# Another written order of the steps, and the second PSUM bank of two inverse quarters taken from the three-bank ring

## The chip, the core and the metric

The kernel runs on one core of a Trainium2 chip. The metric is the time on the device of one execution, in microseconds, as the median of several runs. Five engines run side by side, each through its own list of instructions in a fixed order: TensorE (PE; its weight loads are shown as PEld), VectorE (DVE), ScalarE (ACT), GpSimd (POOL) and SyncE (SP, which here only issues DMAs). An instruction starts when the one before it on its engine lets it and the semaphores that it waits for are there.

## The reference

The input is layer-normed to `xn` (2048 rows of 448), and two branches are added to it. Branch A is a state space layer, done as a long convolution; branch B sends each row to the best of 64 x 64 experts in each of 16 heads.

```
xn  = layernorm(x)
# A: D=448 channels, N=256 states
P   = exp(dt*A[:, :, None] * l)                    # l = 0..2047
K   = einsum("dn,dnl,dn->dl", C, P, dt*B).real
y   = irfft(rfft(pad(xn)) * rfft(pad(K)))[:2048] + xn * Dskip
# B: 16 heads, 64x64 experts, the best one of each head
q   = einsum("nd,dhc->nhc", xn, w_q)
s1, s2 = q[..., :256] @ k1.T, q[..., 256:] @ k2.T
e   = argmax(s1) * 64 + argmax(s2)
act = gelu(einsum("nd,nhd->nh", xn, u[e]))         # the softmax over one candidate is 1
out = x + y + einsum("nh,nhd->nd", act, v[e])
```

## The kernel before

**Scores.** `combine` folds each head's `w_q` with the keys (L916, transposes at L931) into a score matrix `W`. For each of 16 tiles of 128 rows, `score` transposes the normed tile (L1000, evicted at L1003), multiplies it with `W` in four quarters (`sc_p`: L1019, L1030) and finds the best key of each head on DVE: the maximum of a row at L1045, a mask at L1052, a tree of minima at L1062 to L1068. A pair of tiles shares the last small steps, and the indices go through DRAM (L1114, L1121).

**Tables.** `batch` makes the powers of the state space layer for 8 channels: exponentials from PE and ACT (L617, L628), phases on DVE (L653), sines on ACT (L668 to L674), and four products on DVE (L699 to L705, the steps `s4_v`). `products` then takes the sum over the states (`k1`, L721, step `s4_k1`), evicts it (L729; the skip term is added at L732), and transforms it (`k3`, L742, step `s4_k3`) into `VK`, evicted at L746. There are 56 batches.

**Convolution.** `conv` handles the channels in chunks of 128, 128, 128 and 64, each in four quarters of frequencies. In the last chunk a quarter is a product with `g` (`cv1`, L824), a multiplication on DVE (`cv3`, L832, two instructions), the inverse (`cv5`, L876) into two PSUM banks, their eviction (`cv6`, L889, one for each bank) and two stores to DRAM (`cv7`, L895). `final` loads the result back across quarters (L1221), does the last product (`f_p`, L1234), evicts it (L1240) and adds it to the output with a DMA that accumulates (L1245).

**Experts.** For each tile, `experts` gathers 16 pieces of expert rows with an indirect DMA (L1148, POOL's queue), multiplies each with the matching rows of `xn` and sums on DVE (the dots, L1156; the rows come from the DMA at L1138 into four buffers called `xr`), puts the results through a gelu (L1163 to L1172, ACT and DVE in turn), spreads them into a matrix `A` (L1179) and sums the weighted expert rows on PE (L1191, step `e_p`), which also frees the gathered buffers. The sum is evicted (L1198) and added to the output (L1201).

**Order.** Nothing is scheduled at run time. All steps are put into streams (one for each kind of work) and the string `ORDER` names, one character a step, which stream gives the next step. Each engine's list is that order cut to the engine. Buffers are rings: a step takes a slot of a ring (`take`) and a later step gives it back (`give`), first freed, first taken. PSUM has eight banks: the ring `kv` with three (tables, `combine`, `f_p`), the ring `s2` with three (scores, `cv1`, one half of an inverse), and one each for `tp` (transposes, the other half of an inverse) and `po` (experts). 25 buffers of 128 x 1024 named `q` are shared by nearly everything that is loaded or gathered.

Of the kernel before, what the change touches and what calls it, by code (L numbers as in the profile page):

```python
# [89 lines left out]
def ac(n):  # L90
    return 55 + 0.833 * n
# [24 lines left out]
class Plan:  # L116
# [65 lines left out]
    "4414Z44HHH04H114116444242462II2IIII2II2I2I2I222I222222JLJ72HMKHH4H234LML477788ML443K44878M44Z44NI4ICCOPC5N4441DDHE7E77CD"  # L182
    "CHI7I9IIIIIIIIEJ9L7H7DM9FFCEL446CD744EF8JDMK4H79749C7EIC7LF8DE8CF7IDMFDF777897R4N445EII9IEDCFF8I7IR76E4CIFD7444ED4SI7RCF"
    "ESD44FAC499AAIEL848MFDZCCZASHESDHEDFFIEF9HRR9ROHAAaQxZPRISISRRISTURUIIIUIIUJUcIIdSSRRJHGIQxegZbHISGHOShBfHPKISSSTUUUUUUU"
    "UUVWWRRRRXSSRROSSfYYyyQyyPyRySIISfhLySTxfRgQNMRxLJhhRgfIhMUUSSUzUzSUzz!RhROyyyIS#!Izh#hSP$z$%yyyyzz!h#SSg!R#I$$%yyTLRRJh"
    "izUczKUSUzUIUzIhMR!#z#h!$SLU$fz%NRUhMRIzOfUSUIfhzVI!hQSS#SgWIW#SyP!hGTRhcyiiyy$$%Jgxf&RxUxixzzaUiSRNhyzXGhRyzKfy!#Kj#h!S"
    "$z$iUSzRSS%RdOPUyzSzL!SMRyz#U!(hLy#yyTzi$$%hyyykMhiYyieRQUUzizzLy!Rj#zMh#dLiz!$hZHex$%khUSzH!iMZRLblfHM#iLM!HUiUlSgRxhjR"
    "#fiNSihgKf$S$OhfcS%IUIIyyyySIxJhSPUTQUzzIxgLyfNyzUhQRzUhIURIUMhk!U#m#IzLmI!&N$nj$h%zIyyyyyhMRSIhzzynh!liKkYz##!hi$S$SUzz"
    "R%VzgZSINZih!#zh!lyHyHyhHJR1ROSP#m$$%SHfizxJSTgIhhyILIfRzIzgIfWQ!MyLRfhUIW#njIi!zfUhhxmy#US$xcxkUyzU$(zdRizyy%nMiRyyeiSy"
    "h!#li#IL&h!hhIhM$zSj$ySURziISzhRX%zIigIiabiOhkhPgK!R#SShzQhYJlgR#LUf!J$$%UyzyizfZHizUyyTM!SfhNZmR#fYzRS!fSzRmhyVyhWjh#Wz"  # L190
    "$SzRinHH$%hSHk!ny#OKUyIS#SKUjylihIUP!yL$iUMTIhckUNxRL$%IUlUzMLIhg&MRhaILxURmxxKyQzfhISfhUIzzzUSfIgyzyyizfhMRzIiISKh!X#gR"
    "RUy#fh!$S$hdOUIyi%%jzSSSinUhhiPhhmknRibUiyRTJRRiUilyyhehhjgSiSzzUUzzRhhyyfzzUgSUiSySROzQVyShhfPQSk!##gh(hfi!$fJRLj$yyTU%"
    "lfUWkMlcxiUhaRx%yymRLyyySimh&hMLjiUyhhnhniSUiRRgRSUzUxNhzSUWNzMOkhUxzzzzzfh!SyYgfyyPYQ#iSiyS!h#zfL$hz$Rig%%RfRfizzyyzljM"
# [1117 lines left out]
```

## Time and profile before

| what | us |
|---|---|
| median of 3 runs | 757.4 |
| lowest and highest | 754.84 and 757.84 |
| the profiled execution's own time | 760.1 |
| its span, first to last instruction | 758.3 |
| busy in it: PE, DVE, ACT, POOL | 646.2, 659.6, 548.3, 359.9 |

A busy share is an average over stages. The prediction below cuts the span into stretches, looks for the engine that is full in each, and asks which engine waited for which. In a line of a group, the numbers behind the bar are its busy time, the mean length of one in ns, and the idle time of the engine just ahead of it, with what ended most of that. In a timeline the first two numbers are the start and the length, and what stands in brackets is the idle time before and what ended it. "x2" counts instructions.

### The profile page before, as it was taken

Reading aid. Unit: us, or ns where it says so; the run is one execution under the profiler, and the core shown is the slowest. Engines: PE = TensorE matmul, PEld = TensorE weight load, DVE = VectorE, ACT = ScalarE, POOL = GpSimd, SP = SyncE. Lnnn points to the kernel's source line nnn. Section 1 sums busy time; section 2 is a strip of 40 time slices with the busy share of each in tenths; the row PEclk is TensorE's granted clock in tenths of the full one; section 3 lists DMA queues with packets and bytes.
Section 4 is the critical chain, followed back from the end, with each engine's and each line's share of the span. In section 5 each row is a group of like instructions: output and inputs, shape, how many; then the busy total and the mean of one; then the engine's idle time right before and its main releaser. Section 6 shows DMA issues by size and latency. Waiting matters only on the chain.

```text
span 758.3 us, 19601 instructions
## 1 busy us (share of the span) xinstructions
PE 646.2 (85%) x7628; PEld 357.3 (47%) x7628; DVE 659.6 (87%) x1595; ACT 548.3 (72%) x1089; POOL 359.9 (47%) x307
## 2 busy tenths in 40 slices
PE   1999999999998999999899776559997577999892
PEld 0334333344443444443466653336764344676761
DVE  5695557999998999999899999999999989999740
ACT  4686425638896676846668897988889898999630
POOL 2100015653464345554624676786646387616323
PEclk9999999999999999999999997687996776899995
DMA  8999619898988858878997999999989999969889
GB/s 271 331 372 339 233 43 344 268 368 275 330 293 272 244 200 246 247 244 250 306 321 234 319 333 300 323 343 335 301 267 355 276 300 322 258 218 273 298 170 123
DMA packets 118085, 211.29 MB, mean 279 GB/s; under 512 B 38824, under 2 KB 93096, under 8 KB 117928
## 3 DMA queue, kind: packets, MB, share of 16 engines
q0 software_dynamic: 31232, 124.80, 52.2%
q1 hardware_dynamic: 86760, 85.24, 35.4%
q8 instruction: 60, 0.98, 0.5%
q14 instruction: 33, 0.27, 0.1%
HBM read 180.38 MB, written 33.29 MB: 282 GB/s over the span
## 4 chain that ended last, share of the span: by engine, by line
DVE 38%; PE 29%; ACT 15%; DMA 9%; issue 7%; POOL 1%; SPq 1%; POOLq 0%; DVEq 0%; ACTq 0%
PE s L1019 9%; DVE q L1156 9%; DVE mg L705 4%; DVE ph L653 4%; DVE zi L701 4%; PE kv L721 3%; PE kv L916 3%; DMA xr<-xn_d 2%; DVE q L858 2%; ACT CS L668 2%; ACT CS L671 2%; DVE mx L1045 2%; DVE zi L699 2%; ACT CS L674 2%; PE s L1030 2%
## 5 line engine op out<-in xcount | busy, mean ns | idle before, releaser
L1148 POOL DMA_INDIRECT q<-in_uv_dram,ig x256 | 311.9, 1218 | 308.6 <-PE po L1191 93.8
L1019 PE MATMUL s<-q,xt 128*128 128x512 f32 x384 | 178.9, 605 | 3.4 <-ACT xt L1003 2.8
L1156 DVE SCALAR_TENSOR_TENSOR q<-q,xr 128x448 f32<-128x448 f32 x256 | 152.9, 619 | 6.7 <-DMA q<-in_uv_dram,ig 3.7
L1019 PEld LDWEIGHTS s<-q,xt 128*128 128x128 f32 x384 | 69.0, 190 | 92.2 <-issue 85.5
L721 PE MATMUL kv<-mg 128*32 128x64 f32 x1792 | 65.8, 243 | 12.5 <-DVE mg L705 6.9
L1191 PE MATMUL po<-q,A 128*32 128x448 f32 x512 | 67.0, 618 | 10.7 <-DVE A L1179 5.0
L628 ACT ACTIVATE mg<-kv 128x512 f32<-128x512 f32 x112 | 63.5, 604 | 16.4 <-PE kv L617 15.8
L701 DVE TENSOR_TENSOR zi<-mg,CS 128x1024 f32<-128x1024 f32 x56 | 68.4, 1221 | 0.0
L705 DVE TENSOR_TENSOR mg<-mg,CS 128x1024 f32<-128x1024 f32 x56 | 68.2, 1219 | 0.0
L721 PE MATMUL kv<-zi 128*32 128x64 f32 x1792 | 65.7, 240 | 0.2
L668 ACT ACTIVATE CS<-ph 128x1024 f32<-128x1024 int32 x56 | 62.7, 1120 | 3.8 <-DVE ph L653 3.8
L653 DVE CUSTOM_DVE_ANT_0 ph<-st,ph 128x512 uint16<-128x512 uint16 (+2 forms) x84 | 65.1, 775 | 0.2
L674 ACT ACTIVATE CS<-CS,halfpi 128x1024 f32<-128x1024 f32 x56 | 64.5, 1152 | 0.9
L721 PEld LDWEIGHTS kv<-mg 128*32 128x32 f32 x1792 | 47.3, 123 | 33.4 <-issue 14.0
L671 ACT ACTIVATE CS<-ph 128x1024 f32<-128x1024 int32 x56 | 62.7, 1120 | 0.0
L617 PE MATMUL kv<-lc,rt 32*128 32x512 f32 x112 | 39.9, 542 | 26.5 <-ACT mg L628 17.0
L1045 DVE TENSOR_REDUCE mx<-s 128x8 f32<-128x512 f32 x64 | 43.8, 685 | 18.2 <-PE s L1030 13.8
L765 PE MATMUL tp<-q,f 128*128 128x448 f32 x64 | 34.6, 625 | 20.0 <-DMA f<-in_f_dram 14.0
L721 PEld LDWEIGHTS kv<-zi 128*32 128x32 f32 x1792 | 50.2, 125 | 0.8 <-issue 0.7
L881 PE MATMUL s<-q,e 64*128 64x256 f32 x192 | 46.7, 394 | 0.4 <-DVE q L858 0.3
L881 PE MATMUL tp<-q,e 64*128 64x256 f32 x192 | 46.6, 394 | 0.5 <-ACT q L889 0.5
L742 PE MATMUL kv<-f,kt 128*64 128x128 f32 x448 | 38.8, 309 | 9.4 <-ACT mg L628 8.6
(208 smaller groups left out, 1282.4 us busy)
## 6 DMA issues: line engine op xcount, KB each, us to landing
q<-in_wq_dram SPq DMA_DIRECT2D x32, 448.0 KB
xr<-xn_d SPq DMA_DIRECT2D x64, 224.0 KB
vu_d<-q SPq DMA_DIRECT2D x64, 112.0 KB
q<-vu_d SPq DMA_DIRECT2D x12, 512.0 KB
t_d<-q SPq DMA_DIRECT2D x24, 256.0 KB
q<-t_d SPq DMA_DIRECT2D x12, 512.0 KB
q<-in_uv_dram,ig POOLq DMA_INDIRECT x256, 7.1
q<-in_x_dram SPq DMA_DIRECT2D x16, 224.0 KB
```

Source lines behind the costliest of these rows:

```text
L653: s.nc.vector.tensor_tensor(out=rw(n, 2 * n), in0=rw(0, n), in1=o["st"][:, k, b0:b0 + 2].rearrange("p b h m x -> p (b h m x)")[:, None].to ...
L668: s.nc.scalar.activation(CS[:, 1].rearrange("p (m r x) -> p m r x", r=16, x=2), four(s.ph), AF.Sin, scale=SC)
L671: s.nc.scalar.activation(B["CS"][:, 0].rearrange("p (m r x) -> p m r x", r=16, x=2), four(s.ph), AF.Abs)
L674: s.nc.scalar.activation(B["CS"][:, 0], B["CS"][:, 0], AF.Sin, scale=-SC, bias=s.halfpi)
L701: V.tensor_tensor(out=zi[:, 512:], in0=mg[:, 512:], in1=CS[:, 1], op=ALU.mult)
L705: V.tensor_tensor(out=mg[:, 512:], in0=mg[:, 512:], in1=CS[:, 0], op=ALU.mult)
L721: s.nc.tensor.matmul(kp[32 * c:32 * c + 32, 64 * gi:64 * gi + 64], T[ri][:, 1024 + m:1056 + m], view(T[ri], m, [[512, 2], [1, 32]]), start ...
L881: s.nc.tensor.matmul(Q["ip", h][:, 2 * w * x:2 * w * x + 2 * w], s.e[r, k], Q["c", x][r, :, ab, ri], start=(i == 0), stop=(i == 3))
L1019: s.nc.tensor.matmul(B["sc", q].rearrange("p a b -> p (a b)"), B["xt"][:, i], w, start=(q % 2 == 0 and i == 0), stop=(q % 2 == 1 and i == 2))
L1148: s.nc.gpsimd.indirect_dma_start(out=ue, out_offset=None, in_=s.io["uv"], in_offset=bass.IndirectOffsetOnAxis(ap=s.IDX[t][:, c, g:g + 1].b ...
L1156: s.nc.vector.scalar_tensor_tensor(Q["ue", g, c][:, :D], Q["ue", g, c][:, :D], 1.0, B["xr", c], op0=ALU.mult, op1=ALU.mult, accum_out=Q["d ...
L1191: s.nc.tensor.matmul(B["po"][32 * c:32 * c + 32, :D], Q["A"][:, g - g0, c], Q["ue", g, c][:, D:], start=(g == 0), stop=(g == 3))
```

## The change

In the last chunk (`last`), the quarters 1 and 3 take the second bank of their inverse from the ring `kv` instead of `tp`; quarters 0 and 2, and all quarters of the other chunks, are as before. The number of instructions stays as it is, and so does the arithmetic. The string `ORDER` is replaced by another permutation of the same steps; line numbers from there on are two higher (L1191 is now L1193).

```diff
 ORDER = (
-    "4414Z44HHH04H114116444242462II2IIII2II2I2I2I222I222222JLJ72HMKHH4H234LML477788ML443K44878M44Z44NI4ICCOPC5N4441DDHE7E77CD"
+    "041HH4HH222I2II2II22I44I1I4ZI1I41I1IJJ4446H724K22K22222222LMLMHHH4L772M4L678848I5I74834M444CC14ODPDI34444CIEEIDNIIII4Z7C"
...
-            def c5(Q=Q):
+            sec = "kv" if last and q % 2 else "tp"
+
+            def c5(Q=Q, sec=sec):
                 for h in range(2):
-                    Q["ip", h] = s.pst([128, 4 * w], ("s2", "tp")[h], "ip")
+                    Q["ip", h] = s.pst([128, 4 * w], ("s2", sec)[h], "ip")
...
-            m = p.add("cv5", "PE", 36.0 * w, c5, deps=[v, s.C["e"]], take=("i1", "tp", "tq"), give=("cA",) if last else ("cA", "cB"))
+            m = p.add("cv5", "PE", 36.0 * w, c5, deps=[v, s.C["e"]], take=("i1", sec, "tq"), give=("cA",) if last else ("cA", "cB"))
...
-                a = p.add("cv6", "ACT", ac(4 * w), c6, deps=[m], give=(("i1", "tp")[h],))
+                a = p.add("cv6", "ACT", ac(4 * w), c6, deps=[m], give=(("i1", sec)[h],))
```

What this does to the lists is shown at three places.

**PE, the end of the last chunk's inverses.** `L876` (now `L878`) is the inverse of a quarter, `s_` and `tp_` or `kv_` its two banks, `L1191` (now `L1193`) the sum over the last tile's experts, `L1234` (now `L1236`) the last product of the chunk before. Before:

```order
L876 MATMUL tp_110<-q_79,e 128x256
L1191 MATMUL po<-q_96,A 32x448 [waits DMASW1_49]
L1191 MATMUL po<-q_91,A 32x448 [waits DMASW3_49]
L1191 MATMUL po<-q_87,A 32x448 [waits DMASW4_49]
L1191 MATMUL po<-q_98,A 32x448 [waits DMASW5_49]
L1191 MATMUL po<-q_93,A 32x448 [waits DMASW6_49,DVE_49]
L1191 MATMUL po<-q_84,A 32x448 [waits DMASW7_49]
L1191 MATMUL po<-q_103,A 32x448 [waits DMASW0_49]
L1191 MATMUL po<-q_92,A 32x448 [waits DMASW1_49]
L876 MATMUL s_108<-q_101,e 128x256
L876 MATMUL tp_110<-q_101,e 128x256 [waits Activation_49]
```

And now:

```order
L878 MATMUL s_107<-q_92,e 128x256
L878 MATMUL tp_110<-q_92,e 128x256
L1236 MATMUL kv_106<-q_98,q_95 32x128 [waits DMAHW1_49]
L1236 MATMUL kv_106<-q_98,q_95 32x128 x15
L878 MATMUL s_109<-q_99,e 128x256 [waits DVE_49,Activation_49]
L878 MATMUL kv_105<-q_99,e 128x256 [waits Activation_49]
```

Between the third and the fourth inverse there stood eight expert sums; now one last product of the chunk before stands there, and those sums come behind the fourth inverse, which writes a bank of `kv`.

**DVE, the last dots of tile 6.** `L1156` (now `L1158`) is a dot, `L1052`, `L1062` and `L1065` (now two higher) work on scores, `L699` to `L705` are products of the tables. Before, from the 109th to the 112th of the kernel's dots:

```order
L1156 SCALAR_TENSOR_TENSOR q_80,dot<-q_80,xr 128x448 [waits DMASW1_49]
L1156 SCALAR_TENSOR_TENSOR q_87,dot<-q_87,xr 128x448 [waits DMASW2_49]
L1156 SCALAR_TENSOR_TENSOR q_81,dot<-q_81,xr 128x448 [waits DMAHW6_49,DMAHW5_49,DMAHW7_49,DMAHW4_49,DMASW3_49]
L1052 TENSOR_TENSOR q_90<-s_108,mx 128x512 [waits DVE_49,PE_49]
L649 TENSOR_SCALAR ph<-tpl 128x2x2x16 [waits Activation_49]
L649 TENSOR_SCALAR ph<-tpl 128x2x2x16
L732 TENSOR_TENSOR kt<-kv_104,dsk 128x2 [waits Activation_49]
L699 SCALAR_TENSOR_TENSOR zi<-mg,CS 128x512
L1156 SCALAR_TENSOR_TENSOR q_102,dot<-q_102,xr 128x448 [waits DMASW4_49]
```

And now, the same four:

```order
L1158 SCALAR_TENSOR_TENSOR q_99,dot<-q_99,xr 128x448 [waits DMASW7_49]
L1067 TENSOR_TENSOR q_79<-q_79 128x32x32 [waits DVE_49]
L1158 SCALAR_TENSOR_TENSOR q_95,dot<-q_95,xr 128x448 [waits DMAHW2_49,DMAHW1_49,DMAHW7_49,DMAHW0_49,DMASW0_49]
L1158 SCALAR_TENSOR_TENSOR q_80,dot<-q_80,xr 128x448 [waits DMASW1_49]
L1067 TENSOR_TENSOR q_79<-q_79 128x32x16 [waits DVE_49]
L703 TENSOR_TENSOR mg<-mg,CS 128x512
L1158 SCALAR_TENSOR_TENSOR q_88,dot<-q_88,xr 128x448 [waits DMASW2_49]
```

The fourth dot, on `q_88`, now has its gather in a buffer that the first expert sums of the same tile free; before, its buffer came from an older score step.

**DVE, the step from tile 9 to tile 10.** Here the first `xr` buffer is used again: its load for tile 10 can be issued once tile 9's 13th dot is through. `L653` are phases, `L1108`, `L1111`, `L1166` to `L1179` small steps of scores and gelu. Before, the last rows ahead of tile 10's first dot (26 rows stand between the two dots):

```order
L653 ISA ph<-st,ph 128x512 [waits DVE_49]
L1175 TENSOR_TENSOR dw<-dot,ig 128x8
L701 TENSOR_TENSOR zi<-mg,CS 128x1024
L653 ISA ph<-st,ph 128x1024 [waits DVE_49]
L1172 SCALAR_TENSOR_TENSOR th<-th,dw 128x8 [waits DVE_49,Activation_49]
L1179 TENSOR_TENSOR A<-mask,th 128x256 [waits DVE_49]
L703 TENSOR_TENSOR mg<-mg,CS 128x512
L653 ISA ph<-st,ph 128x2048
L705 TENSOR_TENSOR mg<-mg,CS 128x1024
L1156 SCALAR_TENSOR_TENSOR q_103,dot<-q_103,xr 128x448 [waits DMAHW2_49,DMASW1_49]
```

And now, with 20 rows between the two:

```order
L701 TENSOR_TENSOR zi<-mg,CS 128x1024
L1110 RECIPROCAL rcg<-top 128x32
L1168 SCALAR_TENSOR_TENSOR x_4610<-x_4610,dot 128x8 [waits Activation_49]
L653 ISA ph<-ph,st 128x256 [waits DVE_49]
L703 TENSOR_TENSOR mg<-mg,CS 128x512
L653 ISA ph<-st,ph 128x512 [waits DVE_49]
L1177 TENSOR_TENSOR dw<-dot,ig 128x8
L653 ISA ph<-st,ph 128x1024 [waits DVE_49]
L705 TENSOR_TENSOR mg<-mg,CS 128x1024
L1174 SCALAR_TENSOR_TENSOR th<-th,dw 128x8 [waits DVE_49,Activation_49]
L1181 TENSOR_TENSOR A<-mask,th 128x256 [waits DVE_49]
L1158 SCALAR_TENSOR_TENSOR q_84,dot<-q_84,xr 128x448 [waits DMAHW2_49,DMASW0_49]
```

A phase step (`L653` 128x2048) and a set of table products went from ahead of the dot to behind it.

More of the change, by code (lines that the diff above doesn't have):

```diff
@@ new lines @@
+    "IIH74C974FFHIEJLDJCEM5HD97HE6D748LM9F7C8FD74F4E7CN44F4ED4ECIF9787LC8NF4R4C48DMR4ZI4I444EDDC9FECZK4FECZRDFE9I9H7A4HK4H79D"
+    "DILSxI988CHFEMDSIEFF4CEDFEF7RRROIIIQP7Q9IS7SxRNIJxGJ76A7779A7AAABcIaSISSGTUIURRRSUUUSRROSPSSSSTUUUUUUUUIUdeRZRSgIRHHVWWR"
+    "XYyyyyIhIISRROHhSSHIISIyxyIIIYISQPgRIySLbffTRhhgRMILyIRIfMIhfJIUIUISSUUzzzz!#U!hRKROI#ShzSz$fPz$z!hSh#SQ!STy%#hyJhi$$Ryg"
+    "yyy%hyyhRLRMzUUSRSUUfJLUzGUfzRzSRzhUzS!#z#N!$zcQx!SMJhiSO#g!$yS#U$%U$cPVTfiR%RWhyhxgyzyzyyxyxyaUzWNUfUSzR&!SU#f!U#SRhz$h"
@@ L212 @@
+    "phhqiftzi!qgrp#hhpqrxoygfo#ftq!vrp$hfh$k%ixywjhflrsqiixhhhiirklpiij%ghhqhkithhfrliuvpgtqphxmfihqfgrifr&njfzushhhhizhhomo"
+    "hvnthkjmvhiiyztiiilkiu-ljm(iuiynzmynknymyjwwnlzklyywmmyyzyynnzpzzzyyp!pyr#!#$$%rszztrtz)zzrz!##!$$rr)pstt*stut*+(,+))urr"
+    "stt*%%*,%+&,(uu+,)*+,)))*+,*+,*+,")
 class Kernel:
```

47 lines of the change are left out of this document (20 added, 27 removed).

## The prediction

> **What bounds the kernel now.** I read the page first, then the stretches of the span, then DVE's waits. The page's first lines:
>
> ```profile
> span 758.3 us, 19601 instructions
> PE 646.2 (85%) x7628; PEld 357.3 (47%) x7628; DVE 659.6 (87%) x1595; ACT 548.3 (72%) x1089; POOL 359.9 (47%) x307
> ```
>
> PE and DVE are nearly alike over the span, so I cut it where the scores end. The last score matrix product starts at 383 us; in the view by stretches the columns are busy time and count for PE, PEld, DVE, ACT, POOL, then granted clock, DMA share and GB/s:
>
> ```profile
> 383.43 2.84 PE L1019 MATMUL s<-q,xt 128*128 128x512 f32 x6
> ...
> 0.00:20.00 20.00, 3.69 (x4) 1.00 (x4) 10.03 (x35) 8.74 (x21) 5.69 (x17) 1.00 0.86 263
> 20.00:40.00 20.00, 19.01 (x65) 8.15 (x65) 15.11 (x22) 12.13 (x23) 2.08 (x1) 1.00 0.95 336
> 40.00:60.00 20.00, 19.00 (x83) 7.68 (x84) 19.79 (x26) 17.27 (x46) 2.08 (x1) 1.00 1.02 389
> 100.00:140.00 40.00, 38.72 (x119) 15.45 (x120) 29.96 (x78) 18.16 (x48) 18.08 (x16) 1.00 0.70 230
> 140.00:300.00 160.00, 154.45 (x1191) 66.86 (x1190) 154.30 (x432) 115.54 (x254) 78.07 (x70) 1.00 0.85 280
> 300.00:386.00 86.00, 80.89 (x687) 35.87 (x685) 81.88 (x201) 53.06 (x111) 42.72 (x35) 1.00 0.84 268
> 386.00:500.00 114.00, 87.86 (x1545) 60.06 (x1548) 111.83 (x265) 98.08 (x175) 73.47 (x57) 0.88 0.94 305
> 500.00:600.00 100.00, 80.16 (x1412) 56.09 (x1400) 96.69 (x227) 88.39 (x148) 62.28 (x50) 0.84 0.99 315
> 600.00:720.00 120.00, 101.58 (x1934) 73.27 (x1936) 111.30 (x246) 108.69 (x187) 64.14 (x52) 0.85 0.90 276
> 720.00:730.00 10.00, 10.00 (x224) 8.21 (x224) 8.36 (x26) 2.12 (x8) 0.00 (x0) 1.00 0.51 130
> ```
>
> To 140 us PE is full (38.72 of the last 40) and DVE is not (29.96). From 140 to 386 both are: DVE lacks 5.7 and 4.1 us, PE 5.6 and 5.1. From 386 to 720 DVE alone is full: it lacks 2.2, 3.3 and 8.7 us, PE far more. So from 140 us on the span is DVE's work plus DVE's waits, some 24 us of them (5.7 + 4.1 + 2.2 + 3.3 + 8.7), and the new order holds the same work. What it can win or lose is in those 24 us, in the start, and in the tail behind DVE's last work. DVE's waits, in total, times, longest:
>
> ```profile
> DVE kt L732 <- ACT kt L729: 7.1, 7, 3.2
> DVE q L1156 <- DMA q<-in_uv_dram,ig: 3.7, 3, 2.2
> DVE q L1156 <- DMA xr<-xn_d: 2.9, 1, 2.9
> DVE zi L699 <- ACT CS L668: 1.9, 2, 1.3
> ```
>
> **The bank alone: 0.** The group of the fourth bank's products in the last chunk has no idle time ahead of it:
>
> ```profile
> L876 PE MATMUL tp<-q,e 64*128 64x256 f32 x32 | 8.0, 389 | 0.0
> L889 ACT ACTIVATE q<-s 128x256 f32<-128x256 f32 x4 | 1.5, 384 | 11.9 <-PE tp L876 11.9
> ```
>
> PE is busy throughout 720 to 730 with other steps between two inverses, which hide the eviction of `tp`. If that cover went, a quarter would wait for two evictions of 0.38 us; the new list puts quarters 1 and 3 on `kv`, so it cannot go there. Taking a `kv` bank could hold up a last product of the chunk before, which comes behind and has time until the final loads. Both ends near nothing; I take 0. What is left is the order.
>
> **The start: -0.5 (between -1.7 and 0).** PE starts when the matrix `f` is there:
>
> ```profile
> 6.86 0.47 SPq L454 DMA_DIRECT2D pv<-in_A_im_dram  x1
> 11.37 0.36 SPq L307 DMA_DIRECT2D f<-in_f_dram  x1
> 14.00 1.83 PE L765 MATMUL tp<-q,f 128*128 128x448 f32 x2 [14.00 <-DMA f<-in_f_dram]
> ...
> pv<-in_A_im_dram SPq DMA_DIRECT2D x1, 448.0 KB
> ```
>
> The load of `A_im` now stands behind `f`: 448 KB at the 263 GB/s of that stretch are 1.7 us. But from 20 to 60 us the DMA share is 0.95 to 1.02 with the same weights to load, so an early PE meets loads that are not earlier. I take the end nearer to nothing.
>
> **The dots that wait for a gather: +3 (0 to +6.8).** POOL issues a gather when the expert sum has freed its buffer. The time to landing of all 256, its issue, and a sum over four pieces:
>
> ```profile
> DMA to landing us min/median/max: 4.2/7.1/9.4
> ...
> L1148 POOL DMA_INDIRECT q<-in_uv_dram,ig x256 | 311.9, 1218 | 308.6 <-PE po L1191 93.8 <-PE s L1030 54.3 <-issue 39.3
> 724.52 0.96 PE L1191 MATMUL po<-q,A 128*32 128x448 f32 x8
> 375.17 0.62 DVE L1156 SCALAR_TENSOR_TENSOR q<-q,xr 128x448 f32<-128x448 f32 x1 [2.25 <-DMA q<-in_uv_dram,ig]
> ```
>
> I counted, over both written orders, how much DVE work (by the rows) stands between the step that frees a gather's buffer and the dot. The dot at 375.17 is the tightest before, with 4.0 us, and waited 2.25, so some 6.3 us are needed. Below that lie 4 dots before and 6 now, all while scores still run; what they lack, the worst of a cluster counted once, is 2.4 us before (the trace has 3.7) and 5.4 now. The tightest now, with 3.8, is the one on `q_88` in the second place shown: behind the matrix `A` of its own tile PE needs 0.96, POOL 1.2 and the landing 4.2 to 7.1, together 6.4 to 9.3, against some 8.9 us of DVE rows from `A` to the dot, less what PE's backlog delays the sum. With 8 us needed the two counts are 9.2 and 16.0: +6.8. Behind a waiting dot on DVE stand the maxima of scores, whose PSUM banks PE needs for the next ones, and table products; so the wait goes on to PE. As far as PE is late anyway it is hidden, so nothing is the other end. I take 5.4 - 2.4 = 3.
>
> **The loads of `xr`: +1 (0 to +4).** This is the longest wait of a dot, with the load in the chain of waits ahead of it:
>
> ```profile
> 219.90 11.79 DMA xr<-xn_d
> 231.78 0.62 DVE L1156 SCALAR_TENSOR_TENSOR q<-q,xr 128x448 f32<-128x448 f32 x1 [2.86 <-DMA xr<-xn_d]
> ```
>
> A load issued at 219.90 landed 11.8 us later. Between the dot that frees an `xr` buffer and the next that reads it, the least DVE work was 9.2 to 10.3 us, at the four dots of that tile, of which only the last waited; now 7.8 at the same tile's first, 8.0 to 8.4 at the tile two before, 8.5 from tile 9 to 10 (the third place: the 128x2048 phase and table products, 4.7 us, went behind the dot). Most loads thus land sooner than this one. 9.2 - 7.8 = 1.4 more at one place; I take 1, and 4 if all three tiles wait.
>
> **DVE's waits for ACT after the scores: -1 (-3 to +3).** [...]
>
> **The tail: -0.6 (-1.65 to +1).** The chain of waits at the end, with PE's rows:
>
> ```profile
> 719.64 3.02 PE L824 MATMUL s<-VK,q 128*64 128x64 f32 x96 [0.49 <-ACT VK L746]
> 728.42 1.95 PE L1234 MATMUL kv<-q,q 64*32 64x128 f32 x64
> 732.23 1.71 PE L1191 MATMUL po<-q,A 128*32 128x448 f32 x16
> 735.79 0.96 PE L1191 MATMUL po<-q,A 128*32 128x448 f32 x8
> ...
> 737.07 3.77 DMA t_d<-q
> 741.12 4.44 DMA q<-t_d
> ```
>
> From 719.64 PE runs without a gap to the end of the fourth inverse at 735.86. Of that, the eight sums of 1.71 go behind it now: -1.65 if PE stays the bound. But the two last multiplications of DVE, ahead of the last dots before, now stand behind them:
>
> ```profile
> 720.84 1.29 DVE L832 TENSOR_TENSOR q<-q,s 128x512 f32<-128x512 f32 x2 [0.59 <-PE s L824]
> 727.89 0.62 DVE L1156 SCALAR_TENSOR_TENSOR q<-q,xr 128x448 f32<-128x448 f32 x1
> 729.95 0.43 DVE L1179 TENSOR_TENSOR A<-mask,th 128x256 f32<-128x256 f32 x1
> ```
>
> From 720.84 DVE has eight multiplications of 0.61 (4.9), six dots at 0.55 (3.3), a first `A` with its steps (0.6) and, from the last dot's end at 728.43 to 730.38, a gelu's way through ACT (1.95): 10.75, so it ends near 731.6, and the third quarter's pair near 730.4. Inverse (1.93), one last product (0.95), inverse (1.93): 735.2 to 735.3, so -0.6. The sums that were moved cost 1.7 + 0.95 us of PE behind the inverse, under the 8.2 us of the store and the load back.
>
> A rule of the Trainium skill bears here (Runtime: NRT & Kernel Launch, "Instruction fetch mechanics"): instructions are fetched in blocks of 256, mostly hidden. The trace has one gap that nothing else explains:
>
> ```profile
> 715.43 0.32 PE L721 MATMUL kv<-mg 128*32 128x64 f32 x2 [2.36 <-issue]
> ```
>
> If it belongs to a block's edge, as many instructions stand behind it now and it falls into the last table again; if not, 2.4 us could go. No row tells which, and the sum leaves it.
>
> **Sum:** -0.5 + 3 + 1 - 1 - 0.6 = +1.9 us on the profiled span of 758.3 (760.2). That execution took 760.1 us, 2.7 above the median of 757.4, so the median becomes 759.3.
>
> **Rivals.** *Slower, about 763:* the gathers' landing counts nearly in full. The 18 dots with under 8 us then lack 16.0 us against 9.2, and the sum is -0.5 + 6.8 + 1 - 1 - 0.6 = +5.7. It decides once landings come at 7 us where dots are tight. For it: the median of 7.1 and POOL's 93.8 us of waits for expert sums. Against it: before, the same count was 9.2 and the trace had 3.7.
> *Faster, about 751:* ACT reaches the evictions and sines of the tables earlier, and DVE's waits for it after the scores are halved (-7.1 of 14.2), while PE hides half of the 4 us at the dots: 757.4 - 0.5 + 2 - 7.1 - 0.6 = 751.2. It decides once DVE's lack from 386 us on falls by 5. For it: 3.2 of the 7.1 us at L732 were one wait behind the PE gap. [...]
> *No effect, 757.4:* the order's pieces cancel, since DVE's work is the same and the bank was never waited for.
>
> **How the numbers follow.** Half a per cent, 3.8 us, is about what a measurement can tell from no change: under 753.6 is faster, over 761.2 slower. The forecast with its own range of 755 to 764 has 0.47 (0.02 faster, 0.31 the same, 0.14 slower), the slower rival 0.23, the faster 0.22, no effect 0.08. Together: faster 0.24, same 0.39, slower 0.37. The likeliest gives 759.3. The low bounds add to -6.4 (751), the high ones to +14.8 (772), not all at once; I take 751 to 768.
>
> **What would show it.** DVE's waits for gathers at 5 to 8 us in total, the longest at the dots of tile 6; those for `xr` 3 to 5 us, one at tile 3 or 10; DVE's lack from 386 to the first `cv1` (L824) at 12 to 14 us; the fourth inverse ending 15.6 us behind that `cv1`, not 16.2; its two banks without idle time ahead. The forecast is wrong if DVE's lack from 140 us to that `cv1` is under 20 or over 32 us, or if PE's start moves the end of the scores by more than 2 us.

## The result, and the profile after

The changed kernel takes 748.8 us (median of 4 runs, 745.78 to 752.21), beside 757.6 us for the kernel before on the same chip: a ratio of 0.9876, with a 95% interval of 0.9833 to 0.9919. A second comparison, with 10 runs of it and 31 of the kernel before, gives 750.5 against 757.6 us, 0.9924 [0.9892, 0.9956]. (The ratios leave disturbed runs out, so they are not always the quotient of the medians beside them.) The forecast was 759.3 us in a range of 751 to 768: the wrong sign, and both medians lie just under the range.

The profiled execution took 745.78 us. The profile's page of the changed kernel begins so:

```profile
span 744.0 us, 19602 instructions
PE 650.4 (87%) x7628; PEld 357.6 (48%) x7628; DVE 660.3 (89%) x1595; ACT 546.3 (73%) x1087; POOL 374.6 (50%) x307
```

DVE's work is about the same (659.6 us before). The view by stretches of the changed kernel, with the columns as in the prediction (PE, PEld, DVE, ACT, POOL, clock, DMA share, GB/s), its last row cut at the first `cv1`:

```profile
100.00:140.00 40.00, 39.74 (x124) 16.17 (x124) 35.20 (x108) 22.88 (x52) 19.47 (x19) 1.00 0.72 236
140.00:300.00 160.00, 156.39 (x1201) 67.65 (x1200) 154.85 (x431) 113.58 (x257) 79.25 (x68) 1.00 0.86 287
300.00:386.00 86.00, 85.55 (x875) 39.70 (x876) 85.50 (x202) 55.08 (x123) 45.32 (x37) 1.00 0.85 265
...
386.00:704.06 318.06, 265.62 (x4673) 185.15 (x4661) 308.35 (x711) 288.25 (x487) 206.83 (x156) 0.84 0.95 301
```

Two rows differ from before at first sight. In 100 to 140 us DVE does 35.20 us of work in 108 instructions, where it did 29.96 in 78. In 300 to 386 us both DVE and PE are full (85.50 and 85.55 of 86), where they had 81.88 and 80.89. The scores therefore end 9.4 us sooner, as the timeline's last row of a score product shows (383.43 us before):

```profile
374.05 2.84 PE L1021 MATMUL s<-q,xt 128*128 128x512 f32 x6
```

One pair of profiles is one pair of executions, and this pair (760.1 and 745.8 us) lies further apart than the medians. So both kernels were profiled once more, on chips where the kernel before takes 757 us (called quick below; the runs `c_before` and `c_after`, spans 756.7 and 749.0 us). There the last score product starts at 380.9 and 374.1 us, so the scores end 6.8 us sooner. The table gives, for both pairs, the time in each stretch in which DVE did no work, up to the first `cv1`; the two rows below that give how much less work DVE had done by then, and the length of the rest of the span:

| DVE's idle time, us | before | after | c_before | c_after |
|---|---|---|---|---|
| 0 to 100 | 35.10 | 34.79 | 33.42 | 35.02 |
| 100 to 140 | 10.04 | 4.80 | 8.48 | 4.88 |
| 140 to 300 | 5.70 | 5.15 | 3.72 | 4.49 |
| 300 to 386 | 4.12 | 0.50 | 5.86 | 0.83 |
| 386 to the first `cv1` | 14.18 | 9.71 | 14.12 | 15.05 |
| DVE work ahead of that `cv1`, less than before | | 1.39 | | 1.97 |
| length from the first `cv1` to the end | 38.66 | 39.94 | 39.81 | 39.41 |

The first pair's 14.3 us of span are 14.19 of idle time and 1.39 of work, less 1.28 in the tail. The second pair's 7.7 us are 5.33, 1.97 and 0.40. What both share is 100 to 140 us (-5.2 and -3.6) and 300 to 386 us (-3.6 and -5.0), and little else: the 4.5 us that the first pair also gains behind the scores is a loss of 0.9 in the second. From 100 to 140 us, too, the pairs agree less than it seems, for `c_after` lost 1.6 us ahead of that: counted from the start, DVE's idle time to 140 us fell by 5.6 us in the first pair and by 2.0 in the second. From 140 to 386 us it fell by 4.2 and 4.3.

DVE's waits between 100 and 386 us, before (total, times, longest; rows under 0.5 us left out):

```profile
DVE x L1166 <- ACT x L1163: 3.9, 4, 2.1
DVE q L1062 <- ACT q L1057: 3.9, 2, 3.1
DVE q L1156 <- DMA q<-in_uv_dram,ig: 3.7, 3, 2.2
DVE q L1156 <- DMA xr<-xn_d: 2.9, 1, 2.9
DVE mx L1045 <- PE s L1030: 2.5, 3, 1.3
DVE mx L1045 <- PE s L1019: 1.1, 2, 0.9
DVE v L972 <- ACT q L968: 0.6, 1, 0.6
```

And the same view of the changed kernel:

```profile
DVE q L1158 <- DMA q<-in_uv_dram,ig: 3.2, 7, 0.7
DVE x L1168 <- ACT x L1165: 3.1, 3, 1.5
DVE q L1064 <- ACT q L1059: 2.8, 2, 2.2
DVE mx L1047 <- PE s L1032: 1.4, 1, 1.4
DVE mx L1047 <- PE s L1021: 0.5, 1, 0.5
```

All listed waits together fall from 19.4 to 11.2 us (from 19.6 to 10.6 in the second pair), and no single one carries it: `xr` -2.9, the maxima of scores (L1045) -1.7, the tree behind ACT's part of it (L1062) -1.1, the gelu -0.9, the gathers -0.5, the layer norm's `v` -0.6, the rest -0.5.

### The profile page after: what moved, and what is told of

Read it like the earlier page. It is cut to its first block, busy times and chain, and to the rows that moved or that the text cites. A ratio compares the mean times of both kernels' runs of the same rounds, so it can differ in the third digit from the quotient of the medians.

```text
span 744.0 us, 19602 instructions
## 1 busy us (share of the span) xinstructions
PE 650.4 (87%) x7628; PEld 357.6 (48%) x7628; DVE 660.3 (89%) x1595; ACT 546.3 (73%) x1087; POOL 374.6 (50%) x307
## 4 chain that ended last, share of the span: by engine, by line
PE 41%; DVE 19%; ACT 17%; DMA 13%; issue 7%; POOL 2%; SPq 1%; POOLq 0%; DVEq 0%; ACTq 0%
PE s L1021 17%; DMA q<-in_uv_dram,ig 6%; DVE q L1158 4%; PE s L1032 3%; PE po L1193 3%; PE s L846 3%; ACT CS L671 3%; DVE mg L705 3%; ACT CS L668 2%; PE tp L765 2%; PE kv L721 2%; DVE ph L653 2%; DVE zi L701 2%; PE kv L918 2%; DMA hl<-in_h_dram 2%
## 5 line engine op out<-in xcount | busy, mean ns | idle before, releaser
L1150 POOL DMA_INDIRECT q<-in_uv_dram,ig x256 | 325.0, 1270 | 280.8 <-PE po L1193 108.6
L1158 DVE SCALAR_TENSOR_TENSOR q<-q,xr 128x448 f32<-128x448 f32 x256 | 152.5, 617 | 4.3 <-DMA q<-in_uv_dram,ig 4.2
L1193 PE MATMUL po<-q,A 128*32 128x448 f32 x512 | 69.9, 635 | 6.0 <-issue 2.7
L701 DVE TENSOR_TENSOR zi<-mg,CS 128x1024 f32<-128x1024 f32 x56 | 68.1, 1215 | 0.0
L705 DVE TENSOR_TENSOR mg<-mg,CS 128x1024 f32<-128x1024 f32 x56 | 68.0, 1215 | 0.0
L653 DVE CUSTOM_DVE_ANT_0 ph<-st,ph 128x512 uint16<-128x512 uint16 (+2 forms) x84 | 64.9, 773 | 0.2
L617 PE MATMUL kv<-lc,rt 32*128 32x512 f32 x112 | 38.4, 543 | 18.2 <-ACT mg L628 10.4
L1047 DVE TENSOR_REDUCE mx<-s 128x8 f32<-128x512 f32 x64 | 43.6, 681 | 11.1 <-PE s L1032 7.9
L742 PE MATMUL kv<-f,kt 128*64 128x128 f32 x448 | 41.5, 321 | 7.9 <-DVE kt L732 6.2
L883 PE MATMUL s<-q,e 64*128 64x256 f32 x192 | 44.6, 383 | 0.0
L883 PE MATMUL tp<-q,e 64*128 64x256 f32 x192 | 44.6, 382 | 0.0
```

What stands on the lines that cost most here:

```text
L653: s.nc.vector.tensor_tensor(out=rw(n, 2 * n), in0=rw(0, n), in1=o["st"][:, k, b0:b0 + 2].rearrange("p b h m x -> p (b h m x)")[:, None].to ...
L701: V.tensor_tensor(out=zi[:, 512:], in0=mg[:, 512:], in1=CS[:, 1], op=ALU.mult)
L705: V.tensor_tensor(out=mg[:, 512:], in0=mg[:, 512:], in1=CS[:, 0], op=ALU.mult)
L883: s.nc.tensor.matmul(Q["ip", h][:, 2 * w * x:2 * w * x + 2 * w], s.e[r, k], Q["c", x][r, :, ab, ri], start=(i == 0), stop=(i == 3))
L1150: s.nc.gpsimd.indirect_dma_start(out=ue, out_offset=None, in_=s.io["uv"], in_offset=bass.IndirectOffsetOnAxis(ap=s.IDX[t][:, c, g:g + 1].b ...
L1158: s.nc.vector.scalar_tensor_tensor(Q["ue", g, c][:, :D], Q["ue", g, c][:, :D], 1.0, B["xr", c], op0=ALU.mult, op1=ALU.mult, accum_out=Q["d ...
```

## The experiments

Five theories stood against each other. The gain comes from the *head* (the first 100 us or so), from the *middle* of the scores, from the order of the *last two score tiles* (called D where a letter stands), from the *late* part behind the scores (L), or from the *tail* with its other bank (T). In the texts that were written ahead of the runs, S (supply) is the theory that the gain is made before the scores end, head and middle together; O and G say that it comes from the order as a whole, bit by bit, and W that it comes from a few waits. Since both kernels hold the same steps, the two orders can be spliced: the first n steps of one, then the steps that are left, in the sequence of the other. ORDER has 3273 steps; in the changed kernel the 440th is reached on DVE near 122 us, and the 1630th near 368 us, where the last scores are worked on. In the diffs below OLD is the string before, NEW the changed one, and `then(A, B)` stands for A and behind it what is left of B, in B's sequence.

The kernel before needs 832 to 843 us on two of the chips, and 757 on the others. On the slower ones PE pauses among the table products (last section). Neither waits nor ratios carry over from there (the same splice has 1.0050 on such a chip and 0.9914 on a quick one, below), so most of it was run again; `a1_head` and `a3_tables` were not.

**The first splices, on a chip where the kernel before takes 832.1 us.**

```diff
-ORDER = OLD
+ORDER = then(NEW[:440], OLD)       # a1_head
+ORDER = then(NEW[:1630], OLD)      # a2_scores
+ORDER = then(NEW[:3182], OLD)      # a3_tables
+ORDER = then(OLD[:440], NEW)       # b1_oldhead, with the change's ring
```

> The first 440 steps of the new order (some 120 us of the span, to the score products of the fourth tile), the remaining 2833 in the order of before; the ring of before. Theory S (supply: what DVE gets done while PE sets the pace counts to the end, since DVE is the engine that is full later): DVE's idle time to 140 us fell from 45.2 to 39.6 us in the two traces, so this kernel is faster than before by some 5 us (752 to 754), and its first gather is issued near 108.4 us, not 111.2. Rival L (late: the gain is made after the scores, by fewer waits of DVE for ACT): 757.6, within 2 us of before. Rival T (tail): the same as before.

Measured: 831.2 us, 0.9985 [0.9933, 1.0037].

> The first 1630 steps of the new order (to the last score product), the rest as before; the ring of before. Theory S: DVE's lack from 140 to 386 us also falls, from 9.8 to about 5.6 us, and the last score product starts near 374 us, not 383; so 8 to 10 us faster than before (748 to 750). Rival L: the same as before (757). Rival T: the same as before.

Measured: 835.6 us, 1.0050 [1.0005, 1.0096].

> The first 3182 steps of the new order (to just ahead of the last chunk's first product with g), the tail's 91 steps as before, and the ring of before: all of the change but the tail and the bank. Theory S: the last 1500 steps add little, 1 to 4 us; 746 to 749, the tail of the change itself being some 1 us longer than that of before. Rival L: all the gain comes here, 748 to 750 with the two kernels above at 757. Rival T: 757, the gain lying in the tail and the bank.

Measured: 828.0 us, 0.9973 [0.9931, 1.0016].

> The first 440 steps as before, all others in the new order, with the ring of the change: the change without its head. Theory S: the 5 us of the head are missing, 753 to 755; the last score product starts 5 us or so later than in the change (379). Rival L: 749, as the change. Rival T: 749.

Measured: 824.5 us, 0.9925 [0.9888, 0.9962]. By these four the first 1630 steps gain nothing. But on such a chip PE waits elsewhere, as its list of waits in `b1_oldhead` shows; on the quick chips that row comes to 2.0 to 8.3 us, in at most four waits:

```profile
PE kv L721 <- issue: 29.2, 67, 2.3
```

**The same on a chip where the kernel before takes 757.6 us,** with the change itself and the new order without the new ring:

```diff
-            sec = "kv" if last and q % 2 else "tp"
+            sec = "tp"                 # o_order
-ORDER = OLD
+ORDER = then(NEW[:1630], OLD)      # a2_again
+ORDER = then(OLD[:440], NEW)       # b1_again, with the change's ring
```

> The changed kernel itself, beside the parts below on their chip. Where before needs some 757 us: 749, a ratio near 0.988. Where it needs some 830 us and PE's small products (L721) start 0.4 us apart with nothing that they wait for, PE's own rate sets the stretch behind the scores and the gain shrinks: a ratio of 0.99 to 1.00.

Measured: 750.5 us, 0.9924 [0.9892, 0.9956].

> The first 1630 steps of the new order (to the last score product), the rest and the ring as before. Theory S (supply: the gain is made before the scores end): the gain of the change, give or take 2 us; where before needs 757, 748 to 751 and the last score product near 374 us. Rival L (late: the gain is made after the scores): the time of before.

Measured: 749.8 us, 0.9914 [0.9873, 0.9956]. With the old order from step 1630 on, and the old ring, the whole gain is there: the late part (L) and the tail (T) are not needed for it.

> The first 440 steps as before, the others as in the change. Theory S: 4 to 6 us slower than the change (753 to 755 where before needs 757), the last score product 4 to 6 us later than in the change. Rival L: the time of the change (749).

Measured: 751.6 us, 0.9944 [0.9905, 0.9982]. With the old head the kernel is still faster than before; it stands 1.1 us behind the change, within both intervals, and its last score product starts at 374.9 us, 0.8 later than the change's. Theory S had said 4 to 6 us for both, so its part on the head is not borne out: behind the new order of the rest, the first 440 steps are worth little.

> The whole new order, but all quarters of the last chunk take their second bank from tp, as before. All theories but one: the time of the change, within 2 us, since the bank is not waited for. If the bank carries part of the gain: slower than the change, with PE idle ahead of the second and fourth inverse.

Measured: 749.8 us, 0.9908 [0.9868, 0.9948]: the ring does nothing that shows beside intervals of 3 us to either side.

**How far into the middle?** On another quick chip the kernel before was profiled again, and the splice was put at three more places:

```diff
+ORDER = OLD                        # c_before
+ORDER = then(NEW[:800], OLD)       # h800
+ORDER = then(NEW[:1083], OLD)      # h1083
+ORDER = then(NEW[:1460], OLD)      # h1460
```

> The kernel before, profiled again. Its first 440 steps are those of the change without its head, which had its third maximum of scores at 78.8 us where the profile of before has 81.1: if that difference was this one execution's, the maximum comes near 79 us here and the last score product near 381 us (not 383.4); if it is the kernel's, 81 and 383. DVE's wait of 2.9 us for a load of xr near 230 us and of 2.3 us for a gather near 373 us are there again if the order makes them.

Measured: 758.4 us, one run, beside a median of 757.0. The third maximum comes at 79.3 us and the last score product at 380.9, so the 2 us or so by which the first profile was later belonged to that execution. The two waits are there again, but half as long or less: 1.1 us for `xr` and 1.2 for the gather.

> The first 800 steps of the new order (to some 205 us, the middle of tile 7's scores), then before. Two theories on the stretch from 140 to 386 us. W (few waits): the gain is that of the waits seen in before, one of 2.9 us for xr near 230 us, those of 2.3 and 0.5 us for gathers near 375 us, and PE's 2.2 us for DVE near 378 us; so up to step 800 there is little: last score product at 380 to 381, time 755 to 757. G (gradual): the new order packs PE and DVE tighter all along; about a third of the gain: 378 to 379, time 754.

Measured: 756.4 us, 0.9972 [0.9932, 1.0012].

> The first 1083 steps of the new order (to some 270 us, past the place of the long wait for xr), then before. W: the wait for xr at tile 7 is gone and the last score product comes 3 us earlier than with 800 steps, near 377; time 753. G: near 377 too, from 378 to 379 with 800 steps.

Measured: 755.0 us, 0.9959 [0.9916, 1.0003].

> The first 1460 steps of the new order (to some 350 us), then before, the last tiles' gathers and their waits as before. W: as with 1083 steps, within 1 us, the waits near 375 us being still there or moved; the last 3 to 4 us (to 374.5 with 1630 steps) come from the last two tiles. G: 375 to 376, time 751.

Measured: 752.4 us, 0.9934 [0.9899, 0.9969]. The more steps of the new order, the less time; no one splice carries the step from nothing to all, and neighbouring intervals overlap. The last score product came at 383.2, 380.9 and 378.3 us, each time later than theory G had said (378 to 379, near 377, 375 to 376), and theory W's step of 3 us from 800 to 1083 steps was 2.3.

**One wait taken alone.** Two kernels move single steps: `x1_late` is the kernel before with three DVE steps put ahead of its longest waiting gather; `p1_lasttile` has the new order only for what lies between steps 1461 and 1630.

```diff
+L1052 TENSOR_TENSOR q_90<-s_108,mx
+L649 TENSOR_SCALAR ph<-tpl x2
+L699 SCALAR_TENSOR_TENSOR zi<-mg,CS 128x512
 L1156 SCALAR_TENSOR_TENSOR q_87,dot<-q_87,xr
 L1156 SCALAR_TENSOR_TENSOR q_81,dot<-q_81,xr
-L1052 TENSOR_TENSOR q_90<-s_108,mx
-L649 TENSOR_SCALAR ph<-tpl x2
-L699 SCALAR_TENSOR_TENSOR zi<-mg,CS 128x512
...
+ORDER = then(then(OLD[:1461], NEW[:1630]), OLD)    # p1_lasttile, p1_again
```

> The kernel before, with three DVE steps (a mask of scores, a short phase step, a table product, 1.5 us together) moved from behind its 111th dot to ahead of the 110th. Theory D (the dots of tile 6 wait for their gathers at the end of the scores, and the mask queued behind them holds a score bank that PE needs): the waits at the 110th and 111th dot (1.2 and 0.5 us, 2.3 and 0.5 us in the other profile) go, the last score product comes 1.5 to 2.5 us earlier (378.5 to 379.5 against 380.9), and the time falls by 2 us (a ratio near 0.997). Theory O (the order as a whole): the end of the scores moves by under 1 us, 757.

Measured: 841.6 us beside 843.1 on that chip, a ratio of 1.0111 [1.0016, 1.0206]. On a chip of this kind it settles nothing, and it was not repeated on a quick one.

> The first 1461 steps as before, then the new order up to its step 1630 (the last two score tiles), then the rest as before. Theory D (most of the gain lies where the last tiles' scores meet the dots of tile 6): DVE's idle time from 340 to 386 us falls from 4.5 to under 2 us, the last score product comes near 377, and 4 us are gained (753, a ratio of 0.994 to 0.996). Theory O: a fifth of the gain, 1 to 2 us (755.5, ratio 0.998).

Measured: 846.5 us, 1.0168 [1.0109, 1.0227], on the same chip.

> The first 1461 steps as before, then the new order up to its step 1630 (the last two score tiles), then the rest as before. Where before needs some 757 us: theory D (most of the gain lies where the last tiles' scores meet the dots of tile 6) has DVE's idle time from 340 to 386 us at under 2 us (4.5 before), the last score product near 377 (380.9 before) and a ratio of 0.993 to 0.996; theory O (the order as a whole) has a fifth of the gain or nothing: 0.998 to 1.000, the last score product at 379.5 to 381. Where before needs some 840 us, neither can be told.

Measured on a quick chip: 758.5 us, 1.0009 [0.9978, 1.0040]. The last two tiles' new order alone (D) gains nothing: the last score product comes at 380.8 us, and DVE's idle time from 340 to 386 us is 6.7 us. Its listed waits from 100 to 386 us come to 21.1 us (19.4 and 19.6 before), differently shared out; the gathers wait 1.9 us instead of 3.7 and the gelu 8.2 instead of 4.2:

```profile
DVE th L1172 <- ACT th L1169: 4.1, 2, 3.8
DVE x L1166 <- ACT x L1163: 4.1, 4, 2.1
...
DVE q L1156 <- DMA q<-in_uv_dram,ig: 1.9, 2, 1.1
```

**Better than the change?** In `c_after` seven dots of tile 9, behind the scores, wait 8.2 us for their gathers, which `after` did not show (last section). `y1_fill` puts two table products ahead of the first of them, the 154th, and four phase steps ahead of the 158th:

```diff
+L699 SCALAR_TENSOR_TENSOR zi<-mg,CS 128x512
+L701 TENSOR_TENSOR zi<-mg,CS 128x1024
 L1158 SCALAR_TENSOR_TENSOR q_94,dot<-q_94,xr
...
+L649 TENSOR_SCALAR ph<-tpl x2
+L653 ISA ph<-st,ph 128x256
+L653 ISA ph<-st,ph 128x512
+L653 ISA ph<-st,ph 128x1024
 L1158 SCALAR_TENSOR_TENSOR q_101,dot<-q_101,xr
...
-L699 SCALAR_TENSOR_TENSOR zi<-mg,CS 128x512
-L701 TENSOR_TENSOR zi<-mg,CS 128x1024
-L649 TENSOR_SCALAR ph<-tpl x2
-L653 ISA ph<-st,ph 128x256
-L653 ISA ph<-st,ph 128x512
-L653 ISA ph<-st,ph 128x1024
```

> The change, with two table products (1.7 us) moved from behind the 160th dot to ahead of the 154th, and four phase steps (1.5 us) to ahead of the 158th. If the dots 154 to 160 wait 7.5 us in most executions and DVE sets the time there: the waits fall to 4 to 5 us and the time by 2 to 3 us against the change on the same chip (a ratio 0.003 to 0.004 lower). If the waits are rare, or something behind them takes the time back: the time of the change.

Measured: 837.7 us, 0.9936 [0.9875, 0.9998].

> The change itself, beside the others: a ratio of 0.988 to 0.993. Its dots 154 to 160 wait 7 to 8 us if those waits come in most executions, about 1 us if they belonged to the chip of the runs before.

Measured: 838.4 us, 0.9953 [0.9873, 1.0033]. In the profiled executions the waits of those dots are 7.3 us here and 3.7 in `y1_fill`, and the times cannot be told apart.

> The change, with two table products (1.7 us) moved from behind the 160th dot to ahead of the 154th, and four phase steps (1.5 us) to ahead of the 158th. If the dots 154 to 160 wait some 8 us in most executions and DVE sets the time there: the waits fall to 4 to 5 us and the ratio to 0.986 to 0.989 (the change has had 0.988 and 0.992). If something behind them takes the time back: 0.990 to 0.993. If the moved steps have to wait themselves for ACT: no gain either, with DVE's waits for ACT up by what those for gathers fall. Where before needs some 840 us, nothing can be told.

Measured: 823.4 us beside 833.9, 0.9852 [0.9772, 0.9932], again on a slow chip and without the change beside it. Whether this version beats the change stays open.

**What follows.** The runs on quick chips can be put side by side by DVE's busy time between 100 and 386 us. The view by stretches, of `c_before`:

```profile
100.00:386.00 286.00, 277.02 (x2039) 119.94 (x2040) 267.95 (x712) 185.68 (x410) 140.53 (x121) 0.99 0.84 273
```

Of `h1083`:

```profile
100.00:386.00 286.00, 277.93 (x2043) 120.44 (x2044) 269.87 (x725) 186.84 (x415) 138.78 (x121) 0.99 0.84 272
```

Of `a2_again`:

```profile
100.00:386.00 286.00, 280.84 (x2142) 122.98 (x2142) 274.23 (x733) 191.44 (x430) 143.57 (x122) 1.00 0.84 274
```

Of `c_after`:

```profile
100.00:386.00 286.00, 282.02 (x2195) 123.55 (x2197) 275.80 (x739) 191.96 (x430) 144.44 (x123) 1.00 0.84 273
```

And cut at 140 us, of `h800` and then of `b1_again`:

```profile
100.00:140.00 40.00, 39.74 (x124) 16.20 (x124) 35.20 (x109) 22.35 (x50) 20.60 (x19) 1.00 0.75 245
140.00:386.00 246.00, 235.22 (x1869) 102.58 (x1867) 232.00 (x613) 164.48 (x359) 116.58 (x102) 0.98 0.84 274
...
100.00:140.00 40.00, 39.25 (x122) 15.79 (x121) 33.20 (x91) 19.63 (x43) 19.83 (x18) 1.00 0.72 246
140.00:386.00 246.00, 241.92 (x2029) 107.04 (x2027) 240.65 (x633) 168.75 (x378) 125.50 (x105) 1.00 0.86 280
```

| kernel | DVE busy of 286 us | its listed waits | last score product, us | ratio |
|---|---|---|---|---|
| before | 266.2 | 19.4 | 383.4 | 1 |
| c_before | 268.0 | 19.6 | 380.9 | 1 |
| p1_again | 265.6 | 21.1 | 380.8 | 1.0009 [0.9978, 1.0040] |
| h800 | 267.2 | 17.1 | 383.2 | 0.9972 [0.9932, 1.0012] |
| h1083 | 269.9 | 16.6 | 380.9 | 0.9959 [0.9916, 1.0003] |
| h1460 | 272.2 | 14.1 | 378.3 | 0.9934 [0.9899, 0.9969] |
| b1_again | 273.9 | 13.5 | 374.9 | 0.9944 [0.9905, 0.9982] |
| a2_again | 274.2 | 12.4 | 374.5 | 0.9914 [0.9873, 0.9956] |
| c_after | 275.8 | 10.6 | 374.1 | 0.9924 [0.9892, 0.9956] |
| o_order | 275.9 | 10.6 | 374.0 | 0.9908 [0.9868, 0.9948] |

DVE does 6 to 10 us more work before 386 us in the four kernels that are 6 to 8 us faster, and the waits in the list are 6 to 9 us shorter. `a2_again` shows that the first 1630 steps are enough for the gain, and `b1_again` that it needs little of the first 440. So the middle theory stands: the gain is made by the order of the steps from the 440th to the 1630th, from near 122 to near 368 us. No run has the new order between these two alone.

`h800` has the change's 35.20 us of DVE work from 100 to 140 us, but 14.0 us of idle time from 140 to 386 (9.8 and 9.6 before), and its time can't be told from that before; `b1_again` has 5.4 us there, and the gain. That many small waits are the cause is read from the profiles, not tested one by one. PE's busy time from 100 to 386 us rises with DVE's (274.1 and 277.0 us before, 280.8 to 282.0 in the four), so the table does not say which of the two engines held up the other. Nor was it settled which single moves make the gain: the last 170 of these steps alone gain nothing, and the intervals of neighbouring rows overlap.

## Why the prediction was wrong, step by step

**The waits while scores run: the step that failed.** From 140 to 386 us the prediction had two terms, the gathers (+3) and `xr` (+1), and put the maxima of scores, the trees and the gelu at nothing without a reason. So it had DVE waiting 4 us longer there. In its place DVE's idle time from 140 to 386 us fell by 4.2 us in the first pair (9.82 to 5.65) and by 4.3 in the second (9.58 to 5.32). In the lists of waits from 100 to 386 us the gathers went from 3.7 to 3.2 us (second pair 3.6 to 2.9), `xr` from 2.9 and 1.1 to none, and the three kinds without a term from 11.7 to 8.0 (13.8 to 7.7). That is a miss of 8 us, the larger part of the distance from the forecast +1.9 to the measured -8.8 and -7.1.

The tightest place that the prediction named is the 112th dot. The timeline of the changed kernel around it, in the order matrix `A`, sum, gather, dot:

```profile
356.50 0.42 DVE L1181 TENSOR_TENSOR A<-mask,th 128x256 f32<-128x256 f32 x1
357.41 1.71 PE L1193 MATMUL po<-q,A 128*32 128x448 f32 x16
358.62 1.40 POOL L1150 DMA_INDIRECT q<-in_uv_dram,ig  x1 [2.08 <-PE po L1193]
365.74 0.61 DVE L1158 SCALAR_TENSOR_TENSOR q<-q,xr 128x448 f32<-128x448 f32 x1
```

From `A` to the dot are 9.2 us (8.9 predicted), and the dot did not wait: the gather, issued at 358.62, was there within 7.1 us. The forecast had counted 3.8 us of DVE work between the sum and the dot, with 6.3 us needed. But the sum began 0.5 us behind the end of `A`, and from there to the dot were 8.3 us. No dot of tile 6 waits in `after`, where two waited 2.7 us before. So the tightest place had been mis-sized, and the tightest places stood for the whole, while waits of one or two microseconds elsewhere had no price and moved the other way.

**The bound: a stretch left out.** "So from 140 us on the span is DVE's work plus DVE's waits, some 24 us of them … What it can win or lose is in those 24 us, in the start, and in the tail behind DVE's last work." PE is full from 100 to 140 us, and the prediction took DVE's 10.0 idle microseconds there for lost in any order. With PE still full (39.74 us of 40; 38.72 before), they fell by 5.2 us, and by 3.6 in the second pair (5.6 and 2.0 counted from the start). DVE is full later, nearly alone, for 300 us, so work that it does early need not be done then. That this shortens the end is argued, not shown: `h800` has the whole of this gain and loses it again ahead of 386 us, and `b1_again` keeps most of the time's gain with 6.8 us of idle time in this stretch (4.8 in `after`).

**The bank alone, 0: right.** `o_order`, the new order with the old ring, and the change have ratios of 0.9908 and 0.9924 with intervals that nearly coincide, and the fourth inverse has no idle time ahead of its banks (in `after` it starts at 718.42, while the last product before it is still running).

**The start, -0.5 (-1.7 to 0): near nothing, as taken.** PE's timeline, the second group of transposed transforms before, then the first two groups of the changed kernel:

```profile
17.82 1.86 PE L765 MATMUL tp<-q,f 128*128 128x448 f32 x2 [1.99 <-ACT q L768]
...
12.29 1.83 PE L765 MATMUL tp<-q,f 128*128 128x448 f32 x2 [12.29 <-DMA f<-in_f_dram]
18.12 1.86 PE L765 MATMUL tp<-q,f 128*128 128x448 f32 x2 [3.99 <-ACT q L768]
```

PE starts 1.7 us earlier (14.00 before), and the second group stands at 18.12, where it stood at 17.82: nothing is left of it. DVE's idle time to 100 us moved by -0.3 us in one pair and +1.6 in the other. The scores' end did move by more than 2 us, but not through this.

**DVE's waits for ACT after the scores, -1 (-3 to +3): not shown.** No run shows the -1. From 386 us to the first `cv1` DVE lacks 9.7 us in one profile and 15.1 in the other, beside 14.2 and 14.1: the first comes near the faster rival, the second holds 8.2 us of waits for gathers at a place that no term named. Both come from the same kernel.

**The tail, -0.6 (-1.65 to +1): not shown.** +1.3 in one pair, -0.4 in the other. PE's timeline, one row of before, then the changed kernel at the end:

```profile
709.35 0.74 PE L805 MATMUL s<-q,q 128*64 128x64 f32 x19 [0.89 <-issue]
...
696.74 1.03 PE L805 MATMUL s<-q,q 128*64 128x64 f32 x26 [0.31 <-issue]
...
701.33 0.25 PE L721 MATMUL kv<-zi 128*32 128x64 f32 x2 [0.23 <-issue]
...
704.06 2.02 PE L824 MATMUL s<-VK,q 128*64 128x64 f32 x61 [0.48 <-ACT VK L746]
706.87 1.26 PE L824 MATMUL s<-VK,q 128*64 128x64 f32 x35 [0.79 <-issue]
...
720.04 0.38 PE L878 MATMUL kv<-q,e 64*128 64x256 f32 x1
720.35 1.08 PE L1236 MATMUL kv<-q,q 64*32 64x128 f32 x32
...
731.70 4.26 PE L1236 MATMUL kv<-q,q 64*32 64x64 f32 x128 [6.74 <-DMA q<-t_d]
```

The fourth inverse ends 16.4 us behind the first `cv1`, where 15.6 were said and 16.2 stood before; a gap of 0.79 us at 706.87 is as long as the difference from the forecast.

The prediction asked whether the gap of 2.36 us belongs to a block's edge. It does stand at a fixed count of instructions, and it was not alone: before, PE pauses with nothing to wait for at 676 and 548 products from the end of its list (0.89 and 2.36 us), in `c_before` at 548 and 420 (1.93 and 1.44), and in the changed kernel at 674, 547 and 419 (0.31, 0.23 and 0.79). These places are 127 to 128 products apart, each with its weight load, which makes 256 instructions. In the trace's instruction queue (q8, 60 packets of 16 KB in all) one packet starts 2.3 to 2.4 us ahead of the end of each of these pauses. So the traces agree with the blocks of 256 instructions that the Trainium skill names (Runtime: NRT & Kernel Launch, "Instruction fetch mechanics"), and the gap at the old count shrank from 2.36 to 0.23 us. `c_after` has no pause above 0.2 us at these places; what sets their length was not tested.

**The signs that were named.** Gathers at 5 to 8 us, longest at tile 6: 4.2 us, longest 0.7 (and 11.1 in `c_after`, longest at tile 9). `xr` 3 to 5: 0. DVE's lack from 386 us at 12 to 14: 9.7 and 15.1. From 140 us to the first `cv1`, under 20 was to show the forecast wrong: 15.4, and 20.4 in the second profile.

**The rivals.** The faster one, about 751 us, had the size and the wrong place: it put the gain behind the scores, and `a2_again` has all of it with the old order there. The slower one needed landings that decide; `after` has no such wait, and `c_after`, which waits 11.1 us for gathers, is still 7.1 us faster. *No effect* fell with the interval.

## What to carry to other kernels

An order has to be priced over all stages, and over the sum of its small waits rather than at its tightest places. Where one engine is full late, its idle time in an earlier stage that another engine bounds belongs in that sum; work moved into it counts only as far as the stages between do not lose it again. Two orders of the same steps can be spliced, which locates a gain without explaining it. One profile of each is not enough to place a few microseconds: the stretch behind the scores differed by 5 us between two executions of the changed kernel.

## What the runs showed of the chip

**Chips that are ten per cent apart.** The kernel before took 832 to 843 us on two of the chips, and 757 on the others. PE's timeline in `b1_oldhead`, on one of the former:

```profile
404.89 0.28 PE L721 MATMUL kv<-mg 128*32 128x64 f32 x2 [0.47 <-issue]
405.61 0.22 PE L721 MATMUL kv<-mg 128*32 128x64 f32 x1 [0.44 <-issue]
```

Between bursts of the narrow table products PE stood still for some 0.4 us with nothing to wait for, 29 to 45 us in all in the nine profiles from these chips. Most of these pauses come one to five products apart, where the blocks of the section before are 128 apart. Why some chips do that was not settled.

**A gather that took four times as long.** POOL's timeline in `c_after`, two of the gathers for tile 9 and the next:

```profile
452.64 3.43 POOL L1150 DMA_INDIRECT q<-in_uv_dram,ig  x1 [5.88 <-PE po L1193]
456.38 5.45 POOL L1150 DMA_INDIRECT q<-in_uv_dram,ig  x1 [0.30 <-PE kv L721]
462.13 1.43 POOL L1150 DMA_INDIRECT q<-in_uv_dram,ig  x1 [0.30 <-issue]
```

In this profile four out of five take 0.9 to 1.5 us to issue, and none but these two takes more than 3.2. The gathers behind them are issued later, and DVE's timeline has seven dots of the tile that wait, 8.2 us in all; these are the first and the longest:

```profile
476.90 0.63 DVE L1158 SCALAR_TENSOR_TENSOR q<-q,xr 128x448 f32<-128x448 f32 x1 [1.82 <-DMA q<-in_uv_dram,ig]
...
483.43 0.62 DVE L1158 SCALAR_TENSOR_TENSOR q<-q,xr 128x448 f32<-128x448 f32 x1 [2.83 <-DMA q<-in_uv_dram,ig]
```

It came at the same two gathers in six of the nine profiles with the new late order, and not in `after`, `b1_oldhead` and `a3_tables`. While the second ran, DVE did products with two inputs from SBUF back to back (L701 to L705). The Trainium skill says that a DVE instruction with two inputs in SBUF contends with a GpSimd instruction that reads SBUF (SBUF — State Buffer, "Who interferes with whom"). If that slowed these two, the neighbours, which meet the same products, should be slow as well; the three before and the four behind take 1.1 to 2.0 us. So the rule alone doesn't explain it, and no run here does.
